# A decode block with sliding-window attention and a gated FFN: instructions recorded and synchronised by the kernel itself, in 64 KB slots, instead of by a tile framework

## The chip, the cores and the metric

The kernel runs on one core of one Trainium2 chip. The metric is the time of one execution on the device in microseconds, as the median of several runs; smaller is better.

## The reference

Four tokens (one for each of B = 4 sequences, D = 512) go through one transformer block. A conditioning vector c yields six modulation rows. Attention has 32 query heads and 8 key/value heads of 128, and looks at the last 2048 of 8192 cached positions. Everything is float32.

```python
def block(x, k_cache, v_cache, wq, wo, w1, w3, w2, c, w_mod):
    sa, ca, ga, sb, cb, gb = (silu(c) @ w_mod).reshape(4, 6, 1, 512)[:, i]   # i = 0..5
    h = layernorm(x) * (1 + ca) + sa
    q = (h @ wq).reshape(4, 1, 32, 128).transpose(0, 2, 1, 3)
    k, v = (repeat(t[:, :, 8192 - 2048:, :], 4, axis=1) for t in (k_cache, v_cache))
    p = softmax(einsum("bhqd,bhkd->bhqk", q, k) * 128 ** -0.5)
    o = einsum("bhqk,bhkd->bhqd", p, v)
    x = x + ga * (o.transpose(0, 2, 1, 3).reshape(4, 1, 4096) @ wo)
    h = layernorm(x) * (1 + cb) + sb
    return x + gb * ((silu(h @ w1) * (h @ w3)) @ w2)     # w1, w3: 512 x 1792
```

The weights and the cache window come to 101 MB, and each byte is used once.

## The kernel before

The program is written in a tile framework: pools hand out buffers, and the framework orders the instructions of each engine, adds the semaphore waits and closes the program with barriers of all engines (`L363`).

All loads go through one DMA queue, issued by SyncE (SP). The pool `stream` has five slots of 32 KB per partition, and `plan` is the order of the loads: w_mod_a, wq in two halves, then k and v of each of the 8 key/value heads ("groups"), with wo in two halves between them, then the tail: w_mod_b (3 modulation rows), w1, w3 in two pieces, w_mod_c (the sixth row), w2 in four pieces of 8, 4, 1 and 1 blocks of 128 rows. `load_ahead(name)` (`L71` issues) sees to it that a tile's four successors in the plan have been issued too; an issue waits until the last reader of its slot has ended.

The stages:

- Head: transposes' identity and constants, the first norm (`norm`, `modulate`, `transposed`), two modulation rows (`mod_columns`, `L166`).
- `project_q(g)`, eight times: four matmuls of hT with the weights, one per 128 rows of D (`L182`), a scaling on ScalarE (`L184`), four matmuls that add the parts up and transpose (`L187`), a copy into qT (`L188`).
- `group(g)`, eight times: 16 score matmuls (`L211`, four tiles t of 512 positions by four sequences b, each in a 32-column strip of the array), a maximum per tile (`L212`, `L215`), the exponentials on ScalarE (`L225`), 16 transposes (`L235`) and copies (`L236`), 16 value matmuls into o_ps (`L239`), the scaling into o_sb (`L247`, `L248`) and four matmuls that pick out the heads (`L251`, `L252`).
- `project_out(g)` (`L200`) adds a group's product with wo into a_ps: groups 0 to 3 behind group 4, groups 4 to 6 within group 7, group 7 at the end.
- Tail: a_ps is summed into attn (`L264`, `L268`), w_mod_b gives three modulation rows (`L166`, `L167`), the residual and the second norm follow (`L276` to `L158`), then `ffn_in(w1)` (16 matmuls `L290`, copies by ScalarE and VectorE `L294`, `L295`, transposes `L299`), the gate's sigmoid, `ffn_in(w3)`, hidT (`L309`), w_mod_c's matmuls, 56 matmuls with w2 into y_ps (`L318`), two VectorE steps (`L320`, `L321`) and the store of 128 rows, most of them unused (`L322`).

A float32 matmul shows as two passes in the profile, so 16 matmuls are 32 entries. Batch entries stand in rows 0 to 3 of each 32-row strip.

Of the kernel before, what the change touches and what calls it, by code (L numbers as in the profile page):

```python
# [1 line left out]

# [16 lines left out]
ROW = 8192  # L19
SLOTS = 5  # L20
# [3 lines left out]
W3_CUTS = [0, 1, 2]  # L24
EPS = 1e-5


@with_exitstack
def block_kernel(ctx: ExitStack, tc: tile.TileContext, xc_in, w_mod_a, w_mod_b, w_mod_c, wq, k_t, v, wo, w1, w3, w2, out):
# [24 lines left out]
    tiles = {}  # L54

    def load_first():
        t = stream.tile([P, ROW], F32, tag="w", name="w")
        size = w_mod_a.shape[1]
        nc.sync.dma_start(t[:, :size], w_mod_a)
        nc.sync.dma_start(xc_sb, xc_in)  # L60
        tiles["wma"] = t[:, :size]

    def load_ahead(name):

        upto = [n for n, _, _ in plan].index(name) + SLOTS
        for n, src, cuts in plan[len(tiles) : upto]:
            t = stream.tile([P, ROW], F32, tag="w", name="w")
            size = src.shape[1]
            for a, b in zip(cuts[:-1], cuts[1:]) if cuts else ((0, 1),):
                step = size // cuts[-1] if cuts else size  # L70
                nc.sync.dma_start(t[:, a * step : b * step], src[:, a * step : b * step])  # L71
            tiles[n] = t[:, :size]
        return tiles[name]

    def rows(step):

        return B if step else 32

    def bank():
        return ps_t.tile([P, 512], F32, tag="t", name="bank")  # L80

    nc.scalar.preload_act_table_set("natural_log_exp_and_others")
    xc_sb = consts.tile([P, P + 16], F32, name="xc_sb")
    x_sb, ct_sb = xc_sb[:, :P], xc_sb[:, P:]

    load_first()
    wma = load_ahead("wma")


    ident = consts.tile([P, P], F32, name="ident")  # L90
    make_identity(nc, ident)
    same = consts.tile([P, 32], F32, name="same")
    nc.vector.tensor_reduce(same, ident.rearrange("p (j i) -> p i j", i=32), axis=AX.X, op=ALU.add)
    avg = consts.tile([P, 4, 32], F32, name="avg")
    for j in range(4):
        nc.vector.tensor_scalar_mul(avg[:, j, :], same, 1.0 / D)
    avg = avg.rearrange("p j i -> p (j i)")
    pick = consts.tile([P, NC, R, B], F32, name="pick")
    for c in range(NC):
        nc.vector.tensor_copy(pick[:, c], ident.rearrange("p (b i) -> p i b", b=B)[:, c * R : (c + 1) * R, :])  # L100
    eps_t = consts.tile([P, 1], F32, name="eps_t")
    nc.vector.memset(eps_t, EPS)

    o_ps = ps_o.tile([P, 512], F32, name="o_ps")
    nc.vector.memset(o_ps, 0.0)
    a_ps = ps_a.tile([P, 512], F32, name="a_ps")
    nc.vector.memset(a_ps, 0.0)
    hidT = consts.tile([P, NF, 32], F32, name="hidT")
    nc.gpsimd.memset(hidT, 0.0)
    qT = consts.tile([P, G, B, 32], F32, name="qT")  # L110
    nc.gpsimd.memset(qT, 0.0)
    oT = consts.tile([P, G, R, B], F32, name="oT")


    sc = consts.tile([P, 4, 32], F32, name="sc")
    nc.gpsimd.memset(sc, 0.0)
    e = small.tile([P, 16], F32, name="e")
    nc.scalar.activation(e, ct_sb, AF.Exp, scale=-1.0)
    nc.vector.tensor_scalar_add(e, e, 1.0)
    nc.vector.reciprocal(e, e)  # L120
    nc.vector.tensor_mul(sc[:, :, :B], ct_sb.rearrange("p (k b) -> p k b", b=B), e.rearrange("p (k b) -> p k b", b=B))  # L121

    def norm(src, total):

        stat = bank()
        pm, pv = stat[:, 0:1], stat[:, 1:2]
        nc.tensor.matmul(pm, avg, total, start=True, stop=True)  # L127
        xc = work.tile([P, P], F32, name="xc")
        nc.vector.tensor_scalar_sub(xc, src, pm)
# [12 lines left out]
    def modulate(xc, r0, ve, scale1, shift):

        xs = work.tile([P, P], F32, name="xs")
        nc.vector.tensor_mul(xs, xc, scale1)
        a = small.tile([P, 1], F32, name="a")
        nc.vector.scalar_tensor_tensor(a, r0, r0, ve, op0=ALU.mult, op1=ALU.mult)
        r = small.tile([P, 1], F32, name="r")
        nc.vector.scalar_tensor_tensor(r, a, 1.5, r0, op0=ALU.add, op1=ALU.mult)
        h = work.tile([P, P], F32, name="h")  # L150
        nc.vector.scalar_tensor_tensor(h, xs, r, shift, op0=ALU.mult, op1=ALU.add)
        return h

    def transposed(h, name):
        hp = bank()[:, :P]
        nc.tensor.transpose(hp, h, ident)
        hT = consts.tile([P, 4, 32], F32, name=name)
        nc.vector.tensor_copy(hT.rearrange("p j i -> p (j i)"), hp)  # L158
        return hT

    def mod_columns(wv, dst, n):

        pb = bank()
        for k in range(4):
            for j in range(4):
                nc.tensor.matmul(pb[32 * j : 32 * j + rows(k), : n * P], sc[:, k, : rows(k)], wv[:, k, j, :], start=(k == 0), stop=(k == 3))  # L166
        nc.vector.tensor_copy(dst, pb[:, : n * P])  # L167

    tot = small.tile([P, 1], F32, name="tot")
    nc.vector.reduce_sum(tot, x_sb, axis=AX.X)  # L170
    n1 = norm(x_sb, tot)


    mod_a = consts.tile([P, 256], F32, name="mod_a")
    mod_columns(wma.rearrange("p (k j i) -> p k j i", k=4, j=4), mod_a, 2)
    nc.vector.tensor_scalar_add(mod_a[:, P:], mod_a[:, P:], 1.0)
    hT = transposed(modulate(*n1, mod_a[:, P:], mod_a[:, :P]), "hT")

    def project_q(g, wt):
        qp = bank()  # L180
        for k in range(4):
            nc.tensor.matmul(qp[32 * k : 32 * k + 32, :], hT[:, k, :], wt[:, k * 512 : (k + 1) * 512], start=True, stop=True)  # L182
        q_sb = work.tile([P, 512], F32, tag="rows", name="q_sb")
        nc.scalar.mul(q_sb, qp, DH**-0.5)  # L184
# [8 lines left out]
    for half in range(2):
        wq_t = load_ahead(f"wq{half}")
        for i in range(4):
            project_q(4 * half + i, wq_t[:, i * 2048 : (i + 1) * 2048])

    def project_out(g):
        for i in range(R):
            nc.tensor.matmul(a_ps[32 * i : 32 * i + B, :], oT[:, g, i, :], wo_t[:, g % 4, i, :], start=(g == 0), stop=(g == G - 1))  # L200
# [124 lines left out]
def _layout(i):  # L325
    import numpy as np

    def a(t):
        return np.ascontiguousarray(t)
# [38 lines left out]
```

## Time and profile before

| | us |
|---|---|
| median of 3 runs | 245.37 (245.23 to 245.81) |
| the profiled execution | 245.21 |
| its span, first to last instruction | 243.3 |
| PE (matmul) busy | 170.8 (70%) |
| VectorE busy | 51.4 (21%) |
| ScalarE busy | 34.6 (14%) |
| DMA | 101.49 MB, mean 417 GB/s over the span |

Times within the profile count from the start of the span. In the rows of a view, PE is a matmul, PEld the loading of its weights, DVE VectorE, ACT ScalarE, SPq the queue of SyncE. The PE rows contain time in which the array streams at a lower granted clock, so busy does not mean full speed.

### The profile page before, as it was taken

How to read it: one execution, taken by the hardware profiler on the slowest of the kernel's cores; microseconds unless marked ns; L12 is line 12 of the kernel's file. 1: busy time of each engine (PE TensorE's matmuls, PEld its weight loads, DVE VectorE, ACT ScalarE, POOL GpSimd, SP SyncE). 2: the span in 40 equal slices, each digit the busy share in tenths (PEclk: the TensorE clock that was granted, in tenths of full speed). 3: DMA queues.
4: the chain of work that ended last, by engine and by line, in shares of the span. 5: the costliest groups of instructions: out<-in, count | busy, mean ns of one | idle time of the engine just before them, and what ended most of it. 6: DMA issues, size and time to landing. Idle time of an engine off the chain costs nothing.

```text
span 243.3 us, 2816 instructions
## 1 busy us (share of the span) xinstructions
PE 170.8 (70%) x1194; PEld 72.2 (30%) x1194; DVE 51.4 (21%) x163; ACT 34.6 (14%) x90; POOL 2.1 (1%) x9
## 2 busy tenths in 40 slices
PE   0458788787886967885868628838686684766954
PEld 0213353351433332252143102312531230242232
DVE  3230000005143241421231004212411310132210
ACT  2000100100404040040040000400400300100000
POOL 3000000000000000000000000000000000000000
PEclk9999999999999999779578797995795777997999
DMA  7999999999999999999999999999999999999992
GB/s 256 446 431 431 431 431 428 431 431 431 431 424 431 431 428 431 431 431 428 438 431 428 431 431 431 431 428 431 431 436 431 431 434 432 424 427 420 417 415 94
DMA packets 4619, 101.49 MB, mean 417 GB/s; under 512 B 512, under 2 KB 768, under 8 KB 1024
## 3 DMA queue, kind: packets, MB, share of 16 engines
q1 hardware_dynamic: 4608, 101.33, 97.5%
q8 instruction: 9, 0.15, 0.2%
q14 instruction: 2, 0.02, 0.0%
HBM read 101.26 MB, written 0.07 MB: 416 GB/s over the span
## 4 chain that ended last, share of the span: by engine, by line
DMA 66%; PE 28%; ACT 3%; DVE 1%; issue 1%; SPq 0%; ACTq 0%
DMA w<-k_t 30%; DMA w<-v 18%; DMA w<-w 10%; DMA w<-wq 7%; PE s L211 6%; PE bank L182 6%; PE bank L187 6%; PE o_ps L239 5%; PE bank L235 2%; ACT q_sb L184 2%; PE y_ps L318 1%; ACT p_sb L225 1%; DVE mx L212 1%; PE bank L251 0%; PE a_ps L200 0%
## 5 line engine op out<-in xcount | busy, mean ns | idle before, releaser
L211 PE MATMUL s<-w,qT 128*32 128x512 f32 x256 | 41.5, 809 | 15.4 <-DMA w<-k_t 15.4
L235 PE MATMUL bank<-ident,p_sb 128*128 128x128 f32 x128 | 24.4, 341 | 15.4 <-ACT p_sb L225 15.2
L239 PE MATMUL o_ps<-w,pT 128*16 128x512 f32 x256 | 31.2, 630 | 4.6 <-DMA w<-v 4.6
L225 ACT ACTIVATE p_sb<-s,nm 128x512 f32<-128x512 f32 x32 | 21.5, 685 | 82.8 <-DVE nm L215 82.8
L212 DVE TENSOR_REDUCE mx<-s 128x1 f32<-128x512 f32 x32 | 22.1, 692 | 46.2 <-PE s L211 46.2
L235 PEld LDWEIGHTS bank<-ident,p_sb 128*128 128x128 f32 x128 | 18.2, 172 | 26.5 <-ACT p_sb L225 26.4
L211 PEld LDWEIGHTS s<-w,qT 128*32 128x32 f32 x256 | 9.6, 142 | 41.2 <-issue 24.4
L187 PEld LDWEIGHTS bank<-same,q_sb 128*128 128x128 f32 x64 | 14.3, 328 | 19.9 <-ACT q_sb L184 19.9
L187 PE MATMUL bank<-same,q_sb 128*128 128x4 f32 x64 | 15.0, 357 | 6.1 <-ACT q_sb L184 6.1
L182 PE MATMUL bank<-w,hT 128*32 128x512 f32 x64 | 15.5, 1061 | 1.3 <-DMA w<-wq 1.3
L239 PEld LDWEIGHTS o_ps<-w,pT 128*16 128x16 f32 x256 | 6.7, 100 | 24.3 <-issue 18.6
L251 PE MATMUL bank<-pick,o_sb 128*128 128x16 f32 x64 | 9.1, 268 | 5.4 <-ACT o_sb L247 5.4
L248 DVE TENSOR_SCALAR o_sb<-o_ps,rl 128x256 f32<-128x256 f32 x8 | 3.9, 484 | 41.5 <-ACT o_sb L247 41.5
L236 DVE COPY pT<-bank 128x64 f32<-128x64 f32 x32 | 7.2, 225 | 25.0 <-PE bank L235 25.0
L251 PEld LDWEIGHTS bank<-pick,o_sb 128*128 128x128 f32 x64 | 8.3, 190 | 12.8 <-ACT o_sb L247 12.8
L200 PE MATMUL a_ps<-w,oT 128*4 128x512 f32 x64 | 9.2, 714 | 2.4 <-DMA w<-wo 2.2
L247 ACT ACTIVATE o_sb<-o_ps,rl 128x256 f32<-128x256 f32 x8 | 3.8, 474 | 48.5 <-PE o_ps L239 48.5
L184 ACT ACTIVATE q_sb<-bank 128x512 f32<-128x512 f32 x8 | 4.8, 597 | 35.7 <-PE bank L182 35.7
L290 PE MATMUL pg<-w,h2T 128*4 128x512 f32 (+3 forms) x64 | 9.5, 637 | 0.4 <-DVE h2T L158 0.4
L166 PE MATMUL bank<-w,sc 128*4 128x256 f32 (+5 forms) x96 | 9.0, 465 | 0.5 <-DVE sc L121 0.5
L188 DVE COPY qT<-bank 128x64 f32<-128x64 f32 x8 | 1.8, 225 | 35.5 <-PE bank L187 35.5
L127 PE MATMUL bank<-tot,avg 128*128 128x1 f32 x4 | 0.9, 304 | 10.6 <-DVE tot L170 9.1
(75 smaller groups left out, 54.1 us busy)
## 6 DMA issues: line engine op xcount, KB each, us to landing
w<-k_t SPq DMA_DIRECT2D x8, 4096.0 KB, 38.9
w<-v SPq DMA_DIRECT2D x8, 4096.0 KB, 41.4
w<-wq SPq DMA_DIRECT2D x2, 4096.0 KB, 21.4
w<-wo SPq DMA_DIRECT2D x2, 4096.0 KB, 42.4
w<-w SPq DMA_DIRECT2D x1, 3584.0 KB, 39.6
w<-w SPq DMA_DIRECT2D x2, 1792.0 KB, 35.0
w<-w_mod_b SPq DMA_DIRECT2D x1, 3072.0 KB, 40.2
w<-w_mod_a SPq DMA_DIRECT2D x1, 2048.0 KB, 7.8
```

The costliest lines, as they stand in the source:

```text
L166: nc.tensor.matmul(pb[32 * j : 32 * j + rows(k), : n * P], sc[:, k, : rows(k)], wv[:, k, j, :], start=(k == 0), stop=(k == 3))
L182: nc.tensor.matmul(qp[32 * k : 32 * k + 32, :], hT[:, k, :], wt[:, k * 512 : (k + 1) * 512], start=True, stop=True)
L184: nc.scalar.mul(q_sb, qp, DH**-0.5)
L187: nc.tensor.matmul(qtp[:, i, :], q_sb[:, i * P : (i + 1) * P], same[:, :B], start=True, stop=True)
L200: nc.tensor.matmul(a_ps[32 * i : 32 * i + B, :], oT[:, g, i, :], wo_t[:, g % 4, i, :], start=(g == 0), stop=(g == G - 1))
L211: nc.tensor.matmul(s[32 * b : 32 * b + 32, :], q[:, b, :], kv[:, t, b, :], start=True, stop=True)
L212: nc.vector.reduce_max(mx[:, t : t + 1], s, axis=AX.X)
L225: nc.scalar.activation(p_sb[:, t, :], s_t[t], AF.Exp, bias=nm, accum_out=ls[:, t : t + 1])
L235: nc.tensor.transpose(pt[:, c * P : (c + 1) * P], p_sb[:, t, c * P : (c + 1) * P], ident)
L239: nc.tensor.matmul(o_ps[32 * b : 32 * b + NC * R, :], pT[:, t, b].rearrange("p c r -> p (c r)"), vt[:, t, b, :], start=(t == 0), stop=(t = ...
L251: nc.tensor.matmul(otp, o_sb[:, c * P : (c + 1) * P], pick[:, c].rearrange("p r b -> p (r b)"), start=(c == 0), stop=(c == NC - 1))
L290: nc.tensor.matmul(pg[32 * j : 32 * j + rows(k), :n], h2T[:, k, : rows(k)], ws[:, k, j * 512 : j * 512 + n], start=(k == 0), stop=(k == 3))
```

## The change

The kernel no longer uses the tile framework. A class `Program` records every instruction in the order in which it is written, works out from the boxes of memory that they touch which earlier instruction of another engine (or DMA) each must wait for, drops waits that are already implied, and emits each engine's instructions in that order. All instructions are emitted from one line (`L52`). At the end SP waits for the store and clears the semaphores; no barrier of all engines follows.

What else changes:

- Slots: three of 64 KB per partition in place of five of 32 KB. k and v of a group are one transfer (`kv_in[g]`, 128 x 16384), wq is one, wo is one; kv of group 7 comes in two halves. Group g+3's load is written behind group g.
- The tail is three blocks: w_mod_b, which now has four modulation rows, together with w1 (128 x 15360, one transfer, into the slot of group 6), then w3 whole, then w2 in the same four pieces (both into the slot of group 7). The order of the loads is wq, kv0 to kv6, wo, kv7, w_mod_b with w1, w3, w2.
- q: four groups at a time, accumulated over D in PSUM, one scaling and four transposes per half.
- Within a group, heads_out of the group before stands behind the scores, and the value matmuls of a tile behind the transposes of the next. o_sb is scaled by ScalarE alone. project_out of groups 0 to 5 stands ahead of group 7.
- mod_columns gives all four remaining rows at once; w3's matmuls and copies are uncut, ScalarE copies 96 rows of 512 and VectorE 32 of 256.
- The batch stands in every eighth row of a strip, so the store is 16 rows (`res[::8]`); all matmuls take 32 columns of weights where the framework version took 4 for all but the first step.

The core of the diff:

```diff
-    plan = [("wma", w_mod_a, None), ("wq0", wq[0], None), ("wq1", wq[1], None)]
-    for g in range(G):
-        plan += [(f"k{g}", k_t[g], None)]
-        plan += [("wo1", wo[1], None)] if g == G - 1 else []
-        plan += [(f"v{g}", v[g], None)]
-        plan += [("wo0", wo[0], None)] if g == 4 else []
-    plan += [("wmb", w_mod_b, None), ("w1", w1, None), ("w3", w3, W3_CUTS), ("wmc", w_mod_c, None), ("w2", w2, W2_CUTS)]
...
+    ring = sb("ring", 6 * HALF)
+    slots = [ring[:, n * 2 * HALF : (n + 1) * 2 * HALF] for n in range(3)]
...
+    for half in range(2):
+        qp = s_ps[half]
+        for k in range(4):
+            for i in range(4):
+                at = ((half * 4 + i) * 4 + k) * 512
+                do("tensor", "matmul", qp[32 * i : 32 * i + 32, :], hT[:, k, :], wq_t[:, at : at + 512], start=(k == 0), stop=(k == 3))
...
+    def group(g):
+        kt, vt = (kv[g][:, i * HALF : (i + 1) * HALF].rearrange("p (t b n) -> p t b n", t=NT, b=B) for i in range(2))
...
+        if g:
+            heads_out(g - 1)
         for t in range(NT):
+            do("scalar", "activation", p_sb[t], s_ps[t], AF.Exp, bias=nm, accum_out=ls[:, t : t + 1])
+            pt = bank()
...
+            for u in [t - 1] * (t > 0) + [t] * (t == NT - 1):
+                for b in range(B):
+                    do("tensor", "matmul", o_ps[32 * b : 32 * b + NC * R, :], pT[u][:, b].rearrange("p c r -> p (c r)"), vt[:, u, b, :], start=(u == 0), stop=(u == NT - 1))
...
+    for g in range(G - 1):
         group(g)
+        if g < 4:
+            kv[g + 3] = load(slots[(g + 2) % 3], kv_in[g + 3])
+        elif g == 4:
+            wo_t = load(slots[0], wo).rearrange("p (g r n) -> p g r n", g=G, r=R)
+        elif g == 5:
+            kv[7] = slots[1]
+            for i in range(2):
+                load(kv[7][:, i * HALF : (i + 1) * HALF], kv_in[7][:, i * HALF : (i + 1) * HALF])
+    wmb = load(slots[2][:, : w_mod_b.shape[1]], w_mod_b)
+    for g in range(G - 2):
+        project_out(g)
+    group(G - 1)
+    w3_t = load(slots[1][:, : w3.shape[1]], w3)
+    w2_t = slots[1][:, HALF : HALF + w2.shape[1]]
+    step = w2.shape[1] // NF
+    for lo, hi in zip(W2_CUTS[:-1], W2_CUTS[1:]):
+        load(w2_t[:, lo * step : hi * step], w2[:, lo * step : hi * step])
+    project_out(G - 2)
+    heads_out(G - 1)
     project_out(G - 1)
...
-    mod_columns(load_ahead("wmb").rearrange("p (k j i) -> p k j i", k=4, j=4), mod_b, 3)
+    mod_columns(wmb[:, : 4 * 4 * 512].rearrange("p (k j i) -> p k j i", k=4, j=4), mod_b, 4)
...
-        nc.scalar.copy(g_sb[:, :256], pg[:, :256])
-        nc.vector.tensor_copy(g_sb[:96, 256:], pg[:96, 256:])
+        do("scalar", "copy", g_sb[:96], pg[:96])
+        do("vector", "tensor_copy", g_sb[96:, :256], pg[96:, :256])
...
-    gate = ffn_in(load_ahead("w1"))
+    gate = ffn_in(wmb[:, 4 * 4 * 512 :], s_ps[0], p_sb[0])
...
-    nc.sync.dma_start(out, y)
+    do("sync", "dma_start", out, res[::8, :])
+    do.emit()
```

What `Program` does with a recorded instruction, and how it ends the program:

```python
for (name, p0, p1, lo, hi, psum), writes in accesses:
    for (q0, q1, l, h, _), wrote, other in self.touched.get(name, []):
        apart = lo >= h or l >= hi or not (writes or wrote)
        if p0 < q1 and q0 < p1 and not (apart and (not psum or other.engine == engine)):
            if other.engine != engine or other.dma or (wrote and engine != "tensor"):
                key = other if other.dma else other.engine
                latest[key] = max(latest.get(key, other), other, key=lambda o: o.index)
...
made.then_inc(done, 16)                 # made: the store
for engine, sem in cleared.values():
    engine.sem_clear(sem)
nc.sync.wait_ge(done, 16)
nc.sync.sem_clear(done)
```

More of the change, by code (lines that the diff above doesn't have):

```diff
@@ new lines, with box, __init__ @@
+HALF = 8192
+def box(ap):
+    row = 1
+    for n in ap.tensor.shape[1:]:
+        row *= n
+    (step, parts), *free = ap.ap
+    p0, lo = divmod(ap.offset, row)
+    p1, hi = p0 + (parts - 1) * (step // row) + 1, lo + sum((n - 1) * s for s, n in free) + 1
+    if ap.tensor.space == bass.MemoryType.PSUM:
+        return ap.tensor.name, p0 // 32 * 32, -(-p1 // 32) * 32, lo, hi, True
+    return ap.tensor.name, p0, p1, lo, hi, False
+class Op:
+    def __init__(self, engine, emit, waits):
+        self.engine, self.emit, self.waits = engine, emit, waits
+        self.count, self.told = None, False
@@ new lines, in block_kernel, with sb, ps, load @@
+def block_kernel(nc, xc_in, w_mod_a, wq, kv_in, wo, w_mod_b, w3, w2, out):
+    do = Program(nc)
+    def sb(name, *shape):
+        return nc.alloc_sbuf_tensor(name, (P, *shape), F32).ap()
+    def ps(name):
+        return nc.alloc_psum_tensor(name, (P, 512), F32).ap()
+    ring = sb("ring", 6 * HALF)
+    slots = [ring[:, n * 2 * HALF : (n + 1) * 2 * HALF] for n in range(3)]
+    s_ps = [ps(f"s_ps{t}") for t in range(NT)]
+    banks = [ps(f"bank{n}") for n in range(2)]
+    a_ps, o_ps = ps("a_ps"), ps("o_ps")
+    turn = [0]
+    def bank():
+        turn[0] += 1
+        return banks[turn[0] % 2]
+    def load(dst, src):
+        do("sync", "dma_start", dst, src)
+        return dst
+    def batch(t):
+        return t[:, ::8]
@@ L82, in block_kernel @@
     nc.scalar.preload_act_table_set("natural_log_exp_and_others")
-    xc_sb = consts.tile([P, P + 16], F32, name="xc_sb")
+    xc_sb = sb("xc_sb", P + 16)
     x_sb, ct_sb = xc_sb[:, :P], xc_sb[:, P:]
[L86 to L94, printed above, removed]
+    wma = load(slots[0][:, : w_mod_a.shape[1]], w_mod_a)
@@ new lines, in block_kernel @@
+    load(xc_sb, xc_in)
+    wq_t = load(slots[1], wq)
+    kv = [None] * G
+    kv[0] = load(slots[2], kv_in[0])
+    ident = sb("ident", P)
+    do("gpsimd", "memset", ident, 0.0)
+    do("gpsimd", "affine_select", ident, ident, compare_op=ALU.not_equal, fill=1.0, base=0, pattern=[[-1, P]], channel_multiplier=1)
+    sc = sb("sc", 4, 32)
+    do("gpsimd", "memset", sc, 0.0)
+    hidT = sb("hidT", NF, 32)
+    do("gpsimd", "memset", hidT, 0.0)
+    qT = sb("qT", G, B, 32)
+    do("gpsimd", "memset", qT, 0.0)
@@ L95, in block_kernel @@
+    eps_t = sb("eps_t", 1)
+    do("vector", "memset", eps_t, EPS)
+    do("vector", "memset", o_ps, 0.0)
+    do("vector", "memset", a_ps, 0.0)
+    spread = sb("spread", 32)
+    do("vector", "memset", spread, 0.0)
+    same = sb("same", 32)
+    do("vector", "tensor_reduce", same, ident.rearrange("p (j i) -> p i j", i=32), axis=AX.X, op=ALU.add)
+    avg = sb("avg", 4, 32)
     for j in range(4):
-        nc.vector.tensor_scalar_mul(avg[:, j, :], same, 1.0 / D)
+        do("vector", "tensor_scalar_mul", avg[:, j, :], same, 1.0 / D)
@@ L97, in block_kernel @@
     avg = avg.rearrange("p j i -> p (j i)")
-    pick = consts.tile([P, NC, R, B], F32, name="pick")
+    do("vector", "tensor_copy", batch(spread), same[:, :B])
+    pick = sb("pick", NC, R, B)
     for c in range(NC):
[L100 to L105, printed above, removed]
@@ new lines, in block_kernel @@
+    ss, ln, r0, ve, a, r = (sb(n, 1) for n in ("ss", "ln", "r0", "ve", "a", "r"))
+    def norm(src, total):
+        pm, pv = bank()[:, 0:1], bank()[:, 0:1]
+        do("tensor", "matmul", pm, avg, total, start=True, stop=True)
+        do("vector", "tensor_scalar_sub", xc, src, pm)
+        do("vector", "scalar_tensor_tensor", sq, xc, 1.0, xc, op0=ALU.mult, op1=ALU.mult, accum_out=ss)
+        do("tensor", "matmul", pv, avg, ss, start=True, stop=True)
+        do("scalar", "activation", ln, pv, AF.Ln, bias=eps_t)
+        do("scalar", "activation", r0, ln, AF.Exp, scale=-0.5)
+        do("vector", "tensor_scalar", ve, pv, EPS, -0.5, op0=ALU.add, op1=ALU.mult)
@@ L193, in block_kernel @@
[L193 to L196, printed above, removed]
+                do("tensor", "matmul", pb[32 * j : 32 * j + 32, : n * P], sc[:, k, :], wv[:, k, j, :], start=(k == 0), stop=(k == 3))
+        do("vector", "tensor_copy", dst, pb[:, : n * P])
+    tot = sb("tot", 1)
+    do("vector", "reduce_sum", tot, x_sb, axis=AX.X)
+    norm(x_sb, tot)
+    mod_a = sb("mod_a", 256)
+    mod_columns(wma.rearrange("p (k j i) -> p k j i", k=4, j=4), mod_a, 2)
@@ new lines, in block_kernel @@
+    for half in range(2):
+        do("scalar", "mul", work, s_ps[half], DH**-0.5)
+        qtp = bank()
+        for i in range(R):
+            do("tensor", "transpose", qtp[:, i * P : (i + 1) * P], work[:, i * P : (i + 1) * P], ident)
+        for i in range(R):
+            src = qtp[:, i * P : (i + 1) * P].rearrange("p (g q) -> p g q", g=4)[:, :, ::8]
+            do(
+                "vector",
+                "tensor_copy",
+                qT[:, 4 * half : 4 * half + 4, :, i : NC * R : R],
+                src[:, :, :, None].to_broadcast([P, 4, B, NC]),
+            )
@@ L198, in project_out @@
+    kv[2] = load(slots[1], kv_in[2])
     def project_out(g):
         for i in range(R):
[L200 to L207 removed]
+            do("tensor", "matmul", a_ps[32 * i : 32 * i + B, :], oT[:, g, i, :], wo_t[:, g, i, :], start=(g == 0), stop=(g == G - 1))
@@ new lines, in block_kernel, with heads_out @@
+    mx, nm, ls, l, rl = (sb(n, m) for n, m in (("mx", NT), ("nm", 1), ("ls", NT), ("l", 1), ("rl", 1)))
+    p_sb = [sb(f"p_sb{t}", 512) for t in range(NT)]
+    pT = [sb(f"pT{t}", B, NC, R) for t in range(NT)]
+    o_sb = sb("o_sb", 512)
+    def heads_out(g):
+        otp = bank()[:, : R * B]
+        for c in range(NC):
+            do("tensor", "matmul", otp, o_sb[:, c * P : (c + 1) * P], pick[:, c].rearrange("p r b -> p (r b)"), start=(c == 0), stop=(c == NC - 1))
+        do("vector", "tensor_copy", oT[:, g].rearrange("p r b -> p (r b)"), otp)
@@ L226, in group @@
-        l = small.tile([P, 1], F32, name="l")
-        nc.vector.reduce_sum(l, ls, axis=AX.X)
-        rl = small.tile([P, 1], F32, name="rl")
-        nc.vector.reciprocal(rl, l)
-        pT = work.tile([P, NT, B, NC, R], F32, name="pT")
-        for t in range(NT):
+                do("tensor", "matmul", s_ps[t][32 * b : 32 * b + 32, :], qT[:, g, b, :], kt[:, t, b, :], start=True, stop=True)
+            do("vector", "reduce_max", mx[:, t : t + 1], s_ps[t], axis=AX.X)
+        do("vector", "tensor_reduce", nm, mx, axis=AX.X, op=ALU.max, negate=True)
@@ L246, in group @@
-        o_sb = work.tile([P, 512], F32, name="o_sb")
-        nc.scalar.activation(o_sb[:, :256], o_ps[:, :256], AF.Copy, scale=rl)
-        nc.vector.tensor_scalar_mul(o_sb[:, 256:], o_ps[:, 256:], rl)
-        otp = bank()[:, : R * B]
-        for c in range(NC):
-            nc.tensor.matmul(otp, o_sb[:, c * P : (c + 1) * P], pick[:, c].rearrange("p r b -> p (r b)"), start=(c == 0), stop=(c == NC - 1))
-        nc.vector.tensor_copy(oT[:, g].rearrange("p r b -> p (r b)"), otp)
-    wo_t = None
@@ new lines, in group @@
+        do("vector", "reduce_sum", l, ls, axis=AX.X)
+        do("vector", "reciprocal", rl, l)
+        do("scalar", "activation", o_sb, o_ps, AF.Copy, scale=rl)
+    for g in range(G - 1):
+        group(g)
+        if g < 4:
[6 more added lines that the diff above has]
+                load(kv[7][:, i * HALF : (i + 1) * HALF], kv_in[7][:, i * HALF : (i + 1) * HALF])
@@ L264, in block_kernel @@
-    nc.scalar.copy(a_sb[:, :256], a_ps[:, :256])
-    nc.vector.tensor_copy(a_sb[:, 256:], a_ps[:, 256:])
+    do("scalar", "copy", work, a_ps)
     attn = bank()
     for j in range(4):
-        nc.tensor.matmul(attn[32 * j : 32 * j + 32, :P], same, a_sb[:, j * P : (j + 1) * P], start=True, stop=True)
-    mod_b = consts.tile([P, 384], F32, name="mod_b")
-    ga, sb, cb1 = (mod_b[:, i * P : (i + 1) * P] for i in range(3))
-    mod_columns(load_ahead("wmb").rearrange("p (k j i) -> p k j i", k=4, j=4), mod_b, 3)
@@ L273, in block_kernel @@
-    nc.vector.tensor_scalar_add(cb1, cb1, 1.0)
-    x1 = consts.tile([P, P], F32, name="x1")
-    ag = work.tile([P, P], F32, name="ag")
-    nc.vector.tensor_mul(ag, attn[:, :P], ga)
-    tot2 = small.tile([P, 1], F32, name="tot2")
-    nc.vector.scalar_tensor_tensor(x1, ag, 1.0, x_sb, op0=ALU.mult, op1=ALU.add, accum_out=tot2)
-    h2T = transposed(modulate(*norm(x1, tot2), cb1, sb), "h2T")
-    def ffn_in(ws):
+        do("tensor", "matmul", attn[32 * j : 32 * j + 32, :P], spread, work[:, j * P : (j + 1) * P], start=True, stop=True)
@@ new lines, in block_kernel @@
+    mod_b = sb("mod_b", 512)
+    ga, sh, cb1, gb = (mod_b[:, i * P : (i + 1) * P] for i in range(4))
+    mod_columns(wmb[:, : 4 * 4 * 512].rearrange("p (k j i) -> p k j i", k=4, j=4), mod_b, 4)
+    do("vector", "tensor_scalar_add", cb1, cb1, 1.0)
+    x1, ag, tot2 = sb("x1", P), sq, sb("tot2", 1)
+    do("vector", "tensor_mul", ag, attn[:, :P], ga)
+    do("vector", "scalar_tensor_tensor", x1, ag, 1.0, x_sb, op0=ALU.mult, op1=ALU.add, accum_out=tot2)
+    norm(x1, tot2)
+    modulate(cb1, sh)
@@ L285, in ffn_in @@
+    h2T = transposed("h2T")
+    def ffn_in(ws, pg, g_sb):
         ws = ws.rearrange("p (k f) -> p k f", k=4)
-        pg = ps_s.tile([P, 512], F32, tag="s", name="pg")
         for k in range(4):
@@ L289, in ffn_in @@
                 n = min(512, FF - 512 * j)
[L290 to L295 removed]
+                do("tensor", "matmul", pg[32 * j : 32 * j + 32, :n], h2T[:, k, :], ws[:, k, j * 512 : j * 512 + n], start=(k == 0), stop=(k == 3))
+        do("scalar", "copy", g_sb[:96], pg[:96])
+        do("vector", "tensor_copy", g_sb[96:, :256], pg[96:, :256])
         gt = bank()
```

296 lines of the change are left out of this document (124 added, 172 removed).

## The prediction

> **What bounds the kernel now.** I read the page's slices first, to see which resource never rests, then the chain that ended last, then the last 45 us in order of time. Of the slices (40 of 6.08 us each), the granted TensorE clock, the DMA share and the rate:
>
> ```profile
> PEclk9999999999999999779578797995795777997999
> DMA  7999999999999999999999999999999999999992
> GB/s 256 446 431 431 431 431 428 431 431 431 431 424 431 431 428 431 431 431 428 438 431 428 431 431 431 431 428 431 431 436 431 431 434 432 424 427 420 417 415 94
> ...
> DMA 66%; PE 28%; ACT 3%; DVE 1%; issue 1%; SPq 0%; ACTq 0%
> ```
>
> The DMA engines are full from the first slice to the last but one: 101 MB at about 431 GB/s. Nothing that only shortens an engine's work in the middle can pay. What can move the end is the rate, the head, a gap in the queue, or what remains to do behind the last bytes. The end of the chain, in order of time (start, duration, what):
>
> ```profile
> 159.46 44.76 DMA w<-v
> ...
> 204.26 5.27 PE o_ps L239 x32
> ...
> 213.01 25.48 DMA w<-w
> ...
> 238.53 1.28 PE y_ps L318 x40
> 239.81 0.01 issue
> 239.82 0.45 PE y_ps L318 x8
> 240.26 0.02 issue
> 240.29 0.30 DVE y L320
> 240.59 0.02 issue
> 240.62 0.29 DVE y L321
> ```
>
> v7 lands at 159.46 + 44.76 = 204.22. The last matmuls each wait for a piece of w2. So today a transfer sets the end, and only 0.45 + 0.67 us of arithmetic follow it. The issues of the tail loads and the time from issue to landing:
>
> ```profile
> 180.38 11.72 SPq L71 DMA_DIRECT2D w<-w  x3
> 212.63 1.75 SPq L71 DMA_DIRECT2D w<-w  x4
> 240.93 0.35 SPq L322 DMA_DIRECT2D out<-y  x1
> ```
>
> ```profile
> w<-w SPq DMA_DIRECT2D x1, 3584.0 KB, 39.6
> ...
> w<-w SPq DMA_DIRECT2D x1, 2048.0 KB, 23.4
> ...
> out<-y SPq DMA_DIRECT2D x1, 64.0 KB, 1.5
> ```
>
> w1 (3584 KB) lands at 180.38 + 39.6 = 219.98, the first piece of w2 at 212.63 + 23.4 = 236.03. Between them the arithmetic of the tail runs:
>
> ```profile
> 213.76 2.75 PE L166 MATMUL bank<-w,sc 128*32 128x384 f32 x29
> 216.56 0.56 DVE L167 COPY mod_b<-bank 128x384 f32<-128x384 f32 x1 [3.09 <-PE bank L166]
> ...
> 221.71 5.88 PE L290 MATMUL pg<-w,h2T 128*32 128x512 f32 x34 [0.38 <-DVE h2T L158]
> ...
> 226.82 0.37 ACT L294 COPY g_sb<-pg 128x256 f32<-128x256 f32 x1 [6.78 <-PE pg L290]
> ...
> 227.53 0.61 PE L299 MATMUL bank<-ident,g_sb 128*128 128x128 f32 x4
> 228.06 3.63 PE L290 MATMUL pg<-w,h2T 128*32 128x512 f32 x30
> ...
> 233.06 0.21 DVE L309 TENSOR_TENSOR hidT<-eg,bank 128x56 f32<-128x56 f32 x1 [0.48 <-PE bank L299]
> ...
> 236.12 1.96 PE L318 MATMUL y_ps<-w,hidT 128*32 128x128 f32 x64 [2.09 <-DMA w<-w]
> ```
>
> hidT is ready at 233.27, 2.8 us before w2 begins to land: this chain (modulation, norm, w1, w3) is hidden today, but by 2.8 us only, and because w_mod_b is there by 213.
>
> **The tail load, which decides.** Now w_mod_b (with the columns that were w_mod_c) and w1 are one transfer of 128 x 15360 with one semaphore, behind kv7. The first matmul of mod_columns waits for all of it; behind that wait stands everything that PE still has to do. The same bytes lie ahead as ahead of w1's landing before, plus w_mod_c: 128 x 2048 x 4 B = 1.05 MB, 2.4 us at 431 GB/s. So it lands at 219.98 + 2.4 = 222.4, if the rate stays.
>
> The rate: rows of a transfer grow from 32 to 64 KB (60 KB here). Rates with 32 KB rows, and then in a stretch that carries w3's 14 KB rows (the third-last column is the granted clock, the last GB/s):
>
> ```profile
> 60.00:200.00 140.00, 102.39 (x688) 41.04 (x688) 34.57 (x99) 25.58 (x71) 0.00 (x0) 0.84 1.00 431
> ...
> 220.50:228.00 7.50, 6.63 (x39) 1.86 (x39) 1.10 (x4) 0.37 (x1) 0.00 (x0) 0.77 1.00 420
> ```
>
> One of 16 engines moves 32,768 B in 1216 ns at 431 and 14,336 B in 546 ns at 420, so 18,432 B more cost 670 ns. Drawn on, 65,536 B take 2407 ns: 435.6 GB/s, 1.07% faster, 2.0 us over the 83.4 MB that come in such rows (193.5 us). The other ends: nothing, or as much again lost, since no row here is longer than 32 KB. Against the gain, w_mod_b and w1 with rows of 24 and 28 KB took 6.82 MB in 219.98 - 204.22 = 15.76 us, 433 GB/s, no slower than 32 KB rows. Above 24 KB length seems to matter little; I take 0.6 us. The landing is then 221.8.
>
> [...]
>
> From the landing on, step by step. The first bursts start on a cold clock, as these do (after waits of 4.6 us and of some 5 us with three small matmuls; the third has no such wait ahead):
>
> ```profile
> 204.00:209.00 5.00, 4.74 (x32) 0.98 (x32) 0.00 (x0) 0.00 (x0) 0.00 (x0) 0.66 0.96 413
> ...
> 222.00:226.00 4.00, 4.00 (x29) 0.87 (x24) 0.00 (x0) 0.00 (x0) 0.00 (x0) 0.68 1.04 434
> 226.00:230.00 4.00, 4.00 (x34) 1.38 (x32) 1.33 (x4) 0.59 (x2) 0.00 (x0) 1.00 0.96 404
> ```
>
> 1. mod_columns, 16 matmuls of 512 columns instead of 384, behind some 6 us of idle PE. Nearest row: o_ps L239 after its wait, also 16 of 512: 5.27. It ends at 221.85 + 5.27 = 227.1.
> 2. From there to w1's first matmul: before from 216.51 to 221.71, 5.20. The copy of mod_b grows by 128 columns, and xs now stands behind ve on DVE, where before it filled a wait:
>
> ```profile
> L184 ACT ACTIVATE q_sb<-bank 128x512 f32<-128x512 f32 x8 | 4.8, 597 | 35.7 <-PE bank L182 35.7
> ...
> L167 DVE COPY mod_b<-bank 128x384 f32<-128x384 f32 x1 | 0.6, 558 | 3.1 <-PE bank L166 3.1
> ...
> L167 DVE COPY gb<-bank 128x128 f32<-128x128 f32 x1 | 0.3, 293 | 0.8 <-PE bank L166 0.8
> ```
>
> (558 - 293) / 2 = 0.13 more, and 0.2 for xs (0.29, part of it under ACT): 5.53. w1 begins at 232.6.
> 3. w1's 16 matmuls, cold as before: 221.71 to 226.82, 5.1. To 237.7.
> 4. ACT now copies 512 columns at 0.60 (L184's row), DVE's part is beside it; then 0.06 and four transposes at 0.54 up to the next matmul: 1.2. To 238.9.
> 5. w3, landed long before (3.67 MB behind 221.8: 230.5). 30 passes took 3.63, 32 take 3.87. To 242.8.
> 6. Copy 0.60, two hand-overs 0.12, transposes 0.61, hidT 0.21 with its hand-overs 0.1: 1.6. To 244.4.
> 7. y_ps, 112 passes, none waiting for w2 (landed by 239.2): 1.96 / 64 = 31 ns each, 3.5. To 247.9. Whether 4 or 32 columns of weights are used changes nothing: 1.28 / 40 = 32 ns.
> 8. The two DVE steps and the store's issue: 240.26 to 240.93, 0.67. To 248.6.
> 9. Store of 16 rows: 1.5 to landing, as the 128 rows; 0.1 for the clear. Before, from issue to the end of the span: 243.3 - 240.93 = 2.37, of which these waits are a part:
>
> ```profile
> SPq L363 <- DMA out<-y: 0.9, 1, 0.9
> SPq L363 <- PEq L363: 0.6, 2, 0.4
> ```
>
> So the dropped barriers give 2.37 - 1.6 = 0.8, already in the sum. Bounds: 0 to 1.2.
>
> The span becomes 250.2. The profiled execution took 245.21 with a span of 243.3, so 1.9 lie around it, which I leave: **252.1 us**. The profiled execution is 0.16 below the runs' median of 245.37, less than counts here.
>
> **The other parts, at nothing.** *Queue.* A kv slot of 8.39 MB takes 19.5 us. kv of group g+3 is issued when group g has read its slot; kv g+1 and g+2 are then in the queue, or 39 us from group g's landing. A group costs PE 102.39 / 140 x 19.5 = 14.3 us of busy time, with its softmax waits under 20. The cover is 19 us; gone, each us of lateness would cost one. Issues queued behind a waiting one on SP (w3 and w2 behind w_mod_b) are due only at 222. *Head.* wq arrives whole: its first half lands by 18.57 now, the second 4.19 MB or 9.7 us behind it, at 28.2; kv0 at 47.7.
>
> ```profile
> 18.57 1.97 PE bank L182 x8
> ...
> 54.62 4.97 PE s L211 x32
> ```
>
> Today q ends only at 54.6. Eight bursts at 1.97 are 15.8 us at worst, and two scalings with transposes and copies about 2.5 each: q is ready by 49, about with kv0, and kv2 is issued at 44 for a due time of 67. q of four groups at a time thus removes PE work under full DMA: 0. *Group 7.* The transposes of its last two tiles now stand behind the wait for v7: 8 more behind it, 1.7 us, and o_sb in one piece, 0.13. Before, v7 to attn took 204.26 to 213.9; now it ends at about 216, covered by the landing at 221.8 (6 us). heads_out behind the next group's scores, spread's two small DVE steps, strided batch rows, the constants: work beside waits, 0. *w_mod_c's* own matmuls (1.1 us before w2) go, where PE waited anyway.
>
> **Rivals.** *Transfers still set the end* (faster): the chain fits in front of w2 as now. Then only the barriers and the row length show: 245.2 - 0.8 - 0.6 = 243.8. It decides if hidT is ready by 236 instead of 244.4; with one semaphore for 7.9 MB I see no way to 8.4 us. 4%. *Long rows run much faster* (faster): to be 0.3% under the median, 0.74 us, which is what a measurement here can tell from none, the sum must lose 7.5 us beside the 0.6 already in it. Of the 193.5 us that is 4.2%, 450 GB/s; the long window gives 431. 3%. *A shorter chain, still slower*: mod_columns and w1 run at w3's pace (3.87 instead of 5.27 and 5.1, 2.6 less) and rows gain their full 2.0: 248.1. Against it stand 0.66 and 0.68 in both bursts after a wait. 8%. *A colder chain*: w3 pays w1's pace (+1.2), and y_ps half the clock (+3.5): 256.8. y_ps has no long wait ahead; 8%.
>
> [...]
>
> **How the numbers follow.** The forecast has 77%: PE's chain from the landing at 221.8 sets the end. Around 252.1 the landing may move by -1.4 to +2.6 (rows gaining or losing 2.0), the chain by about 1 either way. The range 248.1 to 255.5 takes in the shorter chain and the lossy rows, and leaves out the two faster cases and most of the colder one. Faster 0.06, same 0.02, slower 0.92.
>
> **What would show it.** Right: PE idle for some 6 us ahead of mod_columns, which starts near 222; DMA share near nothing in the last 9 to 10 us; y_ps in one stretch without a DMA wait; the span ending 1.6 us after the store's issue; DMA full without a gap until 239. Step by step, mod_columns at 5.3 and w1 at 5.1 show the cold clock. Wrong: y_ps waiting for w2, w_mod_b landing before 215, or a rate in the middle far from 431.

## The result, and the profile after

| | before | after |
|---|---|---|
| median of the runs, us | 245.38 (245.23 to 246.39, 6 runs) | 251.9 (250.99 to 253.12, 6 runs) |
| ratio to before | | 1.026 (95%: 1.0228 to 1.0292) |
| the profiled execution, us | 245.21 | 253.12 |
| its span, us | 243.3 | 251.7 |
| PE busy, us | 170.8 | 154.6 |

The changed kernel is 2.6% slower, 6.5 us, although PE is busy for 16 us less. In a later comparison (e10, the last of the experiments) it stood at 1.0269 (1.023 to 1.0308).

The slices of the page after (40 of 6.29 us), the DMA share and the rate, and the chain's shares:

```profile
DMA  7999798998999989999899999999999999999700
GB/s 250 460 469 489 344 492 385 448 489 355 479 419 417 489 375 458 430 406 489 385 440 458 396 470 398 437 448 417 411 422 414 456 456 432 398 433 406 292 0 4
...
DMA 70%; PE 23%; DVE 3%; ACT 2%; issue 1%; SPq 0%; ACTq 0%; DVEq 0%
```

Before, the DMA engines were full up to the last slice but one. Now two slices at the end are empty: the transfers end near 239, as before, and the program runs 12 us more. The end of the chain after, in order of time, shows with what:

```profile
179.00 42.79 DMA ring<-w_mod_b
221.78 0.04 issue
221.82 6.41 PE bank L52 x32
...
233.87 5.54 PE s_ps L52 x20
239.41 0.57 ACT p_sb L52
...
240.69 3.64 PE s_ps L52 x20
...
245.65 0.27 DVE hidT L52
245.91 0.04 issue
245.96 3.31 PE s_ps L52 x112
249.27 0.02 issue
249.29 0.30 DVE p_sb L52
```

From 221.78, where w_mod_b with w1 has landed, no further transfer appears in it. y_ps (the x112) runs in one stretch of 3.31 us, where before it waited for pieces of w2. What PE did ahead of the landing, and the store, from the timeline:

```profile
214.14 0.43 PE L52 MATMUL bank<-work,spread 128*32 128x128 f32 x8 [0.71 <-ACT work L52]
...
221.82 6.35 PE L52 MATMUL bank<-ring,sc 128*32 128x512 f32 x32 [7.25 <-DMA ring<-w_mod_b]
...
249.94 0.55 SPq L52 DMA_DIRECT2D out<-p_sb  x1
```

attn is done at 214.57. PE then stands for 7.25 us on one semaphore. The granted clock (third-last column; below, a burst is called cold where it is under 1.00) in the stretches of mod_columns, w1 and w3, and the rate over the middle of the run:

```profile
221.70:228.30 6.60, 6.35 (x32) 1.38 (x32) 0.04 (x1) 0.00 (x0) 0.00 (x0) 0.57 0.98 421
233.80:239.40 5.60, 5.45 (x32) 1.39 (x32) 0.02 (x1) 0.01 (x1) 0.00 (x0) 0.66 0.64 258
240.60:244.30 3.70, 3.65 (x34) 1.08 (x32) 0.91 (x3) 0.22 (x1) 0.00 (x0) 1.00 0.00 0
```

```profile
60.00:200.00 140.00, 97.54 (x644) 32.82 (x640) 28.91 (x81) 22.86 (x59) 0.00 (x0) 0.83 1.00 431
```

### The profile page after: what moved, and what is told of

Read it like the earlier page. It is cut to its first block, busy times and chain, and to the rows that moved or that the text cites. A ratio compares the mean times of both kernels' runs of the same rounds, so it can differ in the third digit from the quotient of the medians.

```text
span 251.7 us, 2538 instructions
## 1 busy us (share of the span) xinstructions
PE 154.6 (61%) x1106; PEld 54.1 (21%) x1106; DVE 47.5 (19%) x155; ACT 33.4 (13%) x84; POOL 2.1 (1%) x9
## 4 chain that ended last, share of the span: by engine, by line
DMA 70%; PE 23%; DVE 3%; ACT 2%; issue 1%; SPq 0%; ACTq 0%; DVEq 0%
DMA ring<-kv_in 53%; DMA ring<-w_mod_b 17%; PE s_ps L52 12%; PE bank L52 7%; PE o_ps L52 5%; ACT p_sb L52 1%; DVE mx L52 1%; SPq L52 0%; DVE mod_b L52 0%; DVE p_sb L52 0%; DVE sq L52 0%; DVE nm L52 0%; DVE h L52 0%; DVE x L52 0%; DVE h2T L52 0%
## 5 line engine op out<-in xcount | busy, mean ns | idle before, releaser
L52 PE MATMUL s_ps<-ring,qT 128*32 128x512 f32 x256 | 44.6, 861 | 39.4 <-DMA ring<-kv_in 39.4
L52 DVE TENSOR_REDUCE mx<-s_ps 128x1 f32<-128x512 f32 x32 | 22.1, 692 | 89.4 <-PE s_ps L52 89.4
L52 PE MATMUL o_ps<-ring,pT 128*16 128x512 f32 x256 | 34.7, 639 | 2.9 <-DMA ring<-kv_in 2.9
L52 ACT ACTIVATE p_sb<-s_ps,nm 128x512 f32<-128x512 f32 x32 | 21.6, 686 | 101.2 <-PE bank L52 84.4
L52 PE MATMUL bank<-ident,p_sb 128*128 128x128 f32 (+1 forms) x136 | 23.8, 302 | 10.5 <-ACT p_sb L52 9.7
L52 PEld LDWEIGHTS s_ps<-ring,qT 128*32 128x32 f32 x256 | 10.1, 151 | 72.9 <-DMA ring<-kv_in 36.7
L52 PEld LDWEIGHTS bank<-ident,p_sb 128*128 128x128 f32 (+1 forms) x136 | 15.5, 150 | 31.7 <-ACT p_sb L52 14.2
L52 PE MATMUL s_ps<-ring,hT 128*32 128x512 f32 x64 | 9.3, 749 | 10.6 <-DMA ring<-wq 10.6
L52 DVE COPY pT<-bank 128x64 f32<-128x64 f32 x32 | 7.2, 225 | 44.2 <-PE bank L52 44.2
L52 PE MATMUL bank<-ring,sc 128*32 128x256 f32 (+1 forms) x64 | 10.0, 801 | 7.3 <-DMA ring<-w_mod_b 7.3
L52 PE MATMUL a_ps<-ring,oT 128*4 128x512 f32 x64 | 10.1, 778 | 5.6 <-DMA ring<-wo 5.3
L52 ACT ACTIVATE o_sb<-o_ps,rl 128x512 f32<-128x512 f32 x8 | 5.5, 688 | 43.3 <-PE o_ps L52 43.3
L52 PE MATMUL s_ps<-ring,h2T 128*32 128x512 f32 (+1 forms) x64 | 9.1, 662 | 0.4 <-DVE h2T L52 0.4
L52 PEld LDWEIGHTS bank<-pick,o_sb 128*128 128x128 f32 x64 | 7.7, 191 | 7.3 <-issue 6.3
L52 PE MATMUL bank<-pick,o_sb 128*128 128x16 f32 x64 | 8.5, 265 | 0.0
L52 PE MATMUL bank<-tot,avg 128*128 128x1 f32 x4 | 1.0, 312 | 11.5 <-DVE tot L52 9.9
L52 PEld LDWEIGHTS o_ps<-ring,pT 128*16 128x16 f32 x256 | 5.1, 96 | 12.5 <-issue 10.0
L52 ACT ACTIVATION_READ_ACCUMULATOR p_sb<-s_ps,nm 128x1 f32 x32 | 6.5, 203 | 0.0
L52 PEld LDWEIGHTS s_ps<-ring,hT 128*32 128x32 f32 x64 | 2.6, 135 | 16.7 <-issue 16.7
L52 DVE COPY qT<-bank 128x64 f32<-128x64 f32 x8 | 2.2, 276 | 20.6 <-PE bank L52 20.3
L52 PEld LDWEIGHTS bank<-ring,sc 128*32 128x32 f32 x64 | 2.8, 167 | 12.9 <-DMA ring<-w_mod_b 7.5
L52 ACT ACTIVATE work<-s_ps 128x512 f32<-128x512 f32 x2 | 1.2, 597 | 25.2 <-PE s_ps L52 21.8
```

Of the source, the lines that this page charges most:

```text
L52: op = Op(engine, lambda: getattr(getattr(self.nc, engine), method)(*args, **kw), [])
```

## The experiments

The theory: the joined transfer of w_mod_b and w1 lands 17 us ahead of the end of the transfers, and behind it stand 28 to 30 us of arithmetic in a row. Rivals: the 64 KB rows or the queue cost rate; the recorder (the class `Program`) and its new instruction order cost time all along. All experiments ran beside the kernel before, whose medians there were 245.30 to 245.37.

**e1: two transfers instead of one.**

```diff
-    wmb = load(slots[2][:, : w_mod_b.shape[1]], w_mod_b)
+    wmb = slots[2][:, : w_mod_b.shape[1]]
+    for lo, hi in ((0, HALF), (HALF, w_mod_b.shape[1])):
+        load(wmb[:, lo:hi], w_mod_b[:, lo:hi])
```

> The changed kernel with one edit: w_mod_b (four rows) and w1 come as two transfers into the same slot, bytes and order unchanged. My theory (the tail is a chain of arithmetic that waits for one 7.9 MB transfer): mod_columns starts when attn is ready, at about 214.6 instead of 221.8, the chain meets w2's landing again (y_ps ends at 239.7 to 240.9), span 242.1 to 243.4, time about 244.0, that is 8 us below the changed kernel and slightly below the kernel before. Rival 1 (the rate with 64 KB rows, or the queue, costs the time): no change, 251.9. Rival 2 (recorded instructions and their new order cost time all along): no change or under 1 us.

Measured: 243.98 (243.18 to 244.57, 8 runs), ratio to before 0.9929 (0.9905 to 0.9952). From its chain in order of time:

```profile
215.30 3.90 PE bank L52 x40
...
224.64 6.32 PE s_ps L52 x20
...
237.51 3.31 PE s_ps L52 x112
```

mod_columns (32 of these 40 entries) follows attn at once, on a PE that has just worked, and takes little more than half of its 6.41 us. The whole loss goes, 7.9 us, and with it both rivals: bytes, rows of the other loads, recorder and instruction order are as they were. w1's burst is now the slow one (6.32). y_ps runs in one stretch and ends at 240.8, late in the expected range, so the chain of arithmetic still ends a little behind w2's landing.

**e2: the same wait in the kernel before.** w_mod_b with all four rows, loaded behind w1, so that mod_columns starts only when both are there; framework, 32 KB slots and barriers stay.

```diff
-    plan += [("wmb", w_mod_b, None), ("w1", w1, None), ("w3", w3, W3_CUTS), ("wmc", w_mod_c, None), ("w2", w2, W2_CUTS)]
+    plan += [("w1", w1, None), ("wmb", w_mod_b, None), ("w3", w3, W3_CUTS), ("w2", w2, W2_CUTS)]
...
-    mod_columns(load_ahead("wmb").rearrange("p (k j i) -> p k j i", k=4, j=4), mod_b, 3)
+    mod_columns(load_ahead("wmb").rearrange("p (k j i) -> p k j i", k=4, j=4), mod_b, 4)
```

> The kernel before, framework, barriers, 32 KB slots and all, with one thing of the change: w_mod_b holds all four rows and is loaded behind w1, so mod_columns can start only when both are there. My theory: it starts at 222.4, and the chain of 29 to 30.5 us behind it gives a span of 251.4 to 252.9 and 253.3 to 254.8 us, at least as slow as the changed kernel. Rivals 1 and 2 (rows of 64 KB, recorder): 245.4, unchanged.

Measured: 253.74 (253.22 to 254.6, 4 runs), ratio 1.0334 (1.0296 to 1.0372). Its chain:

```profile
178.81 43.63 DMA w<-w_mod_b
222.43 0.04 issue
222.48 5.67 PE bank L166 x32
...
245.26 3.31 PE y_ps L315 x112
```

The landing is at 222.43 and the end is again a chain without transfers. The order of the tail loads, with the sixth row moved into w_mod_b, costs 8.4 us, with nothing of the recorder or the slots in it.

**e3: 32 KB rows in the changed kernel.** Each 128 x 16384 load as two halves.

```diff
-        do("sync", "dma_start", dst, src)
+        n = src.shape[1] // 2 if src.shape[1] == 2 * HALF else src.shape[1]
+        for at in range(0, src.shape[1], n):
+            do("sync", "dma_start", dst[:, at : at + n], src[:, at : at + n])
```

> The changed kernel with every 128 x 16384 load (wq, kv, wo) issued as two halves with rows of 32 KB; slots, waits on readers and the tail are unchanged. If long rows gain what I took (0.6 us), it is slower by 0.6: 252.5; by the drawn-out overhead 253.9. If row length above 24 KB does not matter: 251.9 within 0.5. If long rows are slower, it is faster by up to 2.

Measured: 253.36 (251.93 to 253.59, 6 runs), ratio 1.0301 (1.0265 to 1.0336). That overlaps the changed kernel's own interval, since single runs of both spread over about 2 us. Inconclusive by its time, but its trace has mod_columns start at 222.70, 0.9 us later than the changed kernel; e6 repeats it on a quieter base.

**e4: matmuls that keep PE from standing.** They are added in quartets, four matmuls each, and nothing reads their result.

```diff
+    def keep_warm(n):
+        for _ in range(n):
+            for i in range(R):
+                do("tensor", "matmul", o_ps[32 * i : 32 * i + B, :], oT[:, 0, i, :], wo_t[:, 0, i, :], start=True, stop=True)
...
+    keep_warm(7)
     mod_b = sb("mod_b", 512)
...
+    keep_warm(1)
     norm(x1, tot2)
+    keep_warm(2)
```

> The changed kernel with matmuls added whose result nothing reads: seven quartets between attn and mod_columns, one ahead of the second norm's first matmul and two behind its second, so that PE is not idle for long in front of mod_columns and of w1. Theory that the cold clock is a term of the chain: mod_columns falls from 6.4 to about 3.7 and w1 from 5.5 to about 3.8, 3 to 4.5 us in all: about 248. If bursts are slow for another reason (the arriving transfers, the reads of weights): unchanged 251.9, or slower by the added work.

Measured: 248.34 (248.28 to 248.44, 5 runs), ratio 1.0111 (1.0081 to 1.014). mod_columns and w1 in its chain, and the clock in their stretches:

```profile
221.73 3.69 PE bank L52 x32
...
230.94 3.71 PE s_ps L52 x20
```

```profile
221.70:225.45 3.75, 3.72 (x36) 1.15 (x40) 0.01 (x1) 0.00 (x0) 0.00 (x0) 1.00 0.98 421
230.90:234.65 3.75, 3.63 (x32) 1.08 (x32) 0.00 (x0) 0.02 (x1) 0.00 (x0) 1.00 0.93 393
```

With w3's transfer still arriving (421 and 393 GB/s) both bursts run at full clock: arriving data does not slow them. The cold clock is 2.7 and 1.8 us of the changed kernel's profiled chain (6.41 and 5.54).

**e5: the same again**, as a base for the next two.

> The kernel of the warm clock once more, as the base of the next two on the same chip: 248.3, within 0.3.

Measured: 249.87 (248.33 to 250.1, 5 runs); one run at 248.33 and four at 249.7 to 250.1. A miss: what the added matmuls gained did not come in every run. The profiled run is the one at 248.33, so the cause in the other four isn't shown. The mean granted clock of the whole execution doesn't settle it: 0.841 in the run at 248.33, 0.863 to 0.883 in the slower four. e7 has a profile of a longer run.

**e6: e4 with 32 KB rows**, the edit of e3.

> The warm-clock kernel with every 128 x 16384 load issued as two halves with rows of 32 KB. Theory that long rows gain a little (the landing of the tail load was 221.8 with 64 KB rows and 222.4 to 222.7 with 32 KB): 0.6 to 0.9 slower, 249.0. By the drawn-out overhead per row 2.0 slower, 250.3. If row length does not matter: 248.3.

Measured: 249.06 (248.93 to 249.37, 4 runs). Its landing, in the chain:

```profile
222.35 0.04 issue
222.40 3.69 PE bank L52 x32
```

222.35 against 221.69 (e4) and 221.76 (e5): with 64 KB rows the tail load is there 0.6 to 0.7 us earlier, and e6's profiled span (247.6) is 0.6 above e4's and e5's (247.0). The lag is there when wo lands, as the first matmul that waits for the end of wo shows, in e5 and then in e6:

```profile
184.23 8.22 PE L52 MATMUL a_ps<-ring,oT 128*4 128x512 f32 x48 [5.13 <-DMA ring<-wo]
```

```profile
184.82 3.60 PE L52 MATMUL a_ps<-ring,oT 128*4 128x512 f32 x16 [3.82 <-DMA ring<-wo]
```

From there to mod_columns, where the rows of both are alike, both take 37.58 us (221.81 less 184.23, and 222.40 less 184.82). So the cut loads alone make the difference: long rows gain 0.6 us of 222, and not 2.0. A half is also a transfer of its own, so these runs don't separate the length of the rows from the number of transfers.

**e7: e4 with two barriers of all engines behind the store.**

```diff
                 nc.sync.sem_clear(done)
+                nc.all_engine_barrier()
+                nc.all_engine_barrier()
```

> The warm-clock kernel with two barriers of all engines behind the store, as a framework's end has. The store's issue to the end of the span grows from 1.76 toward 2.37, 0.6; if what lies around the span (1.9 before, 1.4 after) belongs to it too, 1.1 in all: 248.9 to 249.4. Rival, that the end of the program costs the same with and without: 248.3.

Measured: 249.51 (249.39 to 250.87, 5 runs). In the profiled execution (250.87, span 249.0), the store's issue, SP's waits, and two pieces of the chain:

```profile
246.62 0.56 SPq L52 DMA_DIRECT2D out<-p_sb  x1
```

```profile
SPq L138 <- DMA out<-p_sb: 1.1, 1, 1.1
...
SPq L140 <- PEq L140: 0.3, 1, 0.3
SPq L139 <- PEq L139: 0.2, 1, 0.2
```

```profile
228.54 2.51 PE o_ps L52 x16
...
231.84 4.25 PE s_ps L52 x20
```

The medians don't show the cost, since e5's was 249.87; the profile does. From the issue to the end of the span are 2.38 us (e5: 1.75), and the time around the span is 1.8 to 1.9 in its five runs where e4 has 1.3 to 1.4. The barriers cost 0.6 within the span and 0.5 around it. The last two rows are what e5's slower runs may look like: the added matmuls themselves met a cold clock (0.71 over 228.4 to 231.1) and took 2.51 instead of e4's 1.83, held up the transpose behind them, and w1 took 4.25 instead of 3.71.

**e8: e1 with w3 in two pieces and the added matmuls around the second norm.**

> The changed kernel with w_mod_b and w1 as two transfers, w3 in two pieces, and the added matmuls of the warm clock around the second norm only (their result is read by nothing). Theory: w1's burst falls from 6.3 to 3.7, y_ps meets w2's last landing at about 238.9 and ends at 239.4, span 241.8, 243.1 us, 2.2 below the kernel before. Rival (the split kernel already ran at the transfers' end): no gain on its 244.0.

Measured: 243.55 (243.28 to 244.23, 5 runs), ratio 0.9919 (0.9906 to 0.9933). w1's burst was at full clock (32 passes in 3.63 us, as in e4 at 1.00) and y_ps started with w2's first piece, but took 4.86 us; the timeline, then the clock in that stretch:

```profile
235.50 4.86 PE L52 MATMUL s_ps<-ring,hidT 128*32 128x128 f32 x112 [1.72 <-DMA ring<-w]
```

```profile
235.40:236.50 1.10, 1.00 (x20) 1.03 (x24) 0.00 (x0) 0.00 (x0) 0.00 (x0) 0.51 1.03 412
236.50:237.50 1.00, 1.00 (x28) 1.00 (x24) 0.00 (x0) 0.00 (x0) 0.00 (x0) 0.50 0.71 274
237.50:238.50 1.00, 1.00 (x27) 1.00 (x22) 0.00 (x0) 0.00 (x0) 0.00 (x0) 0.50 0.46 176
```

In this execution the burst that could now follow the transfers ran at half clock instead. The median is 0.4 us under e1's, where 0.9 was expected, and the runs of e1 and e8 overlap, so a gain over e1 isn't shown. Both medians lie under those of both kernels: 0.7 to 0.8% under the kernel before, with intervals that leave out 1.

**e9: added matmuls up to y_ps**, one quartet between w3's pieces and two ahead of y_ps.

> The split kernel with w3 in two pieces and added matmuls (read by nothing) around the second norm, between w3's pieces, and two quartets ahead of y_ps, where the split kernel's y_ps ran at a clock of 0.50 from 235.4 to 238.5. If the cold clock still holds y_ps, it now follows w2's landing: last piece at about 239.1, y_ps ends at 239.5 instead of 240.4, 242.6 us. If the transfers already set the end there: unchanged, 243.5.

Measured: 244.72 (243.32 to 245.92, 12 runs), ratio 0.9952 (0.9927 to 0.9977). A miss. From the timeline of its profiled execution (245.52):

```profile
222.15 2.91 PE L52 MATMUL o_ps<-ring,oT 128*4 128x512 f32 x16
...
224.99 0.48 PE L52 MATMUL bank<-ident,h 128*128 128x128 f32 x1
...
236.77 1.90 PE L52 MATMUL o_ps<-ring,oT 128*4 128x512 f32 x16
...
236.87 0.26 DVE L52 TENSOR_TENSOR hidT<-eg,bank 128x56 f32<-128x56 f32 x1 [0.87 <-PE bank L52]
...
238.48 3.24 PE L52 MATMUL s_ps<-ring,hidT 128*32 128x128 f32 x112
```

y_ps is warm here (3.24), but it began 3 us behind w2's first landing in e8. The two quartets around the norm, which e8 has too (1.90 us there), took 2.91, so the transpose that was due by 223.7 (h's last step starts at 223.34 and takes 0.35) ran at 224.99. The two ahead of y_ps took 1.90, as those in e8, and still cost time: hidT was ready at 237.13, and y_ps began at 238.48, behind them. PE ran its matmuls in the order in which they were written, so work added to keep it warm was work on the chain, most of all where it ran slowly all the same (2.91). Five of the twelve runs lie at 243.3 to 243.8, like e8, and seven, the profiled one among them, at 244.7 to 245.9.

**e10: the changed kernel again**, beside e9.

> [...]

Measured: 252.85 (251.19 to 253.56, 6 runs), ratio 1.0269 (1.023 to 1.0308): two runs at 251.2 to 251.3 and four at 252.9 to 253.6. Its profiled execution (252.90) has 6.41 and 5.54 for mod_columns and w1 again.

## Why the prediction was right, step by step

| step | predicted | profiled after |
|---|---|---|
| landing of w_mod_b with w1 | 221.8 | 221.78 |
| mod_columns | 5.27 | 6.41 |
| to w1's first matmul | 5.53 | 5.64 |
| w1 | 5.1 | 5.54 |
| copies, transposes | 1.2 | 1.28 |
| w3 | 3.87 | 3.64 |
| to y_ps | 1.6 | 1.63 |
| y_ps | 3.5 | 3.31 |
| to the store | 0.67 | 0.67 |
| store to the end of the span | 1.6 | 1.76 |
| span | 250.2 | 251.7 |
| around the span | 1.9 | 1.4 |

*The mechanism* is shown from both sides: e2 makes mod_columns of the kernel before wait for w1 too (+8.4 us), e1 takes that wait out of the changed one (-7.9). The parts also add up: 253.74 in e2, less 1.1 for the barriers (e7) and 0.6 for the rows (e6), is 252.0, against 251.9 and 252.85 measured for the changed kernel. What is left for q, the group's new order and the recorder together is under 1 us, inside the spread of the runs.

*Mis-sized terms.* mod_columns was 1.1 us longer in the profiled execution: the nearest row had a granted clock of 0.66 over 5 us, this one 0.57 over 6.6 us. Other runs were up to 2 us shorter than the profiled one; that their cold bursts ended sooner is likely, but none of them was profiled. The store took 1.7 us to landing, not 1.5, and 1.76 to the end of the span; the 0.1 for the clear is shown by no row. The time around the span was left at 1.9 and was 1.4: half a microsecond of the barriers' cost lay outside the span, which e7 shows. The longer mod_columns and the shorter time around the span have opposite signs, so the 0.2 us between forecast and median are partly luck; the sum is good to about 1.5.

*The rate.* 0.6 us was taken between 2.0 and a loss; e6 measured 0.6 to 0.7, and e3's trace has 0.9. The argument from w_mod_b's and w1's 24 and 28 KB rows beat the line drawn through 14 and 32 KB. Over 60 to 200 both kernels show 431 GB/s, a row too coarse for a gain of 0.3%. No run here shows what holds the rate at 431.

*What was costed at nothing.* kv0 landed at 48.44 by the chain (47.7 predicted), the scores began at 48.57, and over 60 to 200 the DMA share is 1.00 at 431 GB/s; no gap shows in the queue. Work behind v7 ended at 214.57, 7 us ahead of the landing.

*The rivals.* Neither faster case came. "Transfers still set the end" fell with y_ps in one stretch, but e1 shows how near it lay: its price of 243.8 is e1's 243.98 within a run's spread. "A shorter chain", priced at 248.1 with 2.6 for the clock, is close to what e4 makes by hand (248.34), but from other terms: more from the clock, and no 2.0 from the rate. "A colder chain" with y_ps at half clock did not happen here; in e8 y_ps ran so for 3 us.

## What to carry to other kernels

In a kernel that streams at full rate, time the arithmetic that follows each of the last transfers and compare it with the transfers still behind that one: here 28 to 30 us stood against 17, and joining two loads under one semaphore cost 8 us while the bytes came in as fast as before. Split the last loads where their readers differ, and order them by the length of what hangs on them, not by how they fill a slot. Less work on an engine (here 16 us on PE) and fewer barriers (1.1 us) show only where they lie on the chain that ends last: the barriers did, the 16 us did not.

## What was not expected of the hardware

The granted clock of a burst depends on more than the wait right ahead of it. In e8 y_ps ran at 0.50 for 3 us after a wait of 1.72, with shorter bursts and waits before that; PE was busy for 2.50 of the 6.06 us ahead (1.92 and 0.58, between waits of 1.06, 0.78 and 1.72). The kernel before starts y_ps after a wait of 2.09, and there the burst is warm (1.00, 64 passes in 1.96 us). Programs that are alike up to that point took different times for the same two quartets: by the chain 1.83 us in e4 and e5 and 2.51 in e7, where the clock was 0.71, by the timeline 1.90 in e8 and 2.91 in e9. That fits the 1.5 to 2.6 us by which single runs of the changed kernel, e5 and e9 differ; the two values of e5 were not profiled side by side, so for that spread the clock is the likely cause and not a shown one. No run here shows what sets the granted clock.
